# A gated mix of an S4 convolution and a routed FFN: a new order of the operations, and more, shorter idle matmuls at the start

## The chip, the core and the metric

The kernel runs on one core of a Trainium2 chip. The metric is the device time of one execution in microseconds. The engines are named as in the profile: PE (TensorE, matmuls; PEld is its weight load), DVE (VectorE), ACT (ScalarE), POOL (GpSimd) and SP (SyncE, which here only issues DMAs). "SPq" and "POOLq" are the DMA queues of SP and POOL. L574 is line 574 of the kernel before; where a line of the changed kernel is meant, that is said.

## The reference

```python
x = A_u                                             # 1 x 2048 x 512, bf16
g = sigmoid((x * gate_w).sum(-1, keepdims=True))
# a: S4 long convolution, D = 512 channels, N = 128 complex modes, L = 2048
dt = exp(log_dt)[:, None]; A = A_re + 1j * A_im
dB = dt * (B_re + 1j * B_im)
P = exp((dt * A)[:, :, None] * arange(L))
K = einsum("dn,dnl,dn->dl", C_re + 1j * C_im, P, dB).real
a = irfft(rfft(u, 2 * L) * rfft(K, 2 * L))[:L] + u * Dskip
# b: the two tokens with the largest x @ w_r go through a SwiGLU FFN
r = x @ w_r; idx = argsort(-r)[:2]; xs = x[idx]
y = (silu(xs @ w_gate) * (xs @ w_up)) @ w_down      # 512 -> 1792 -> 512
b = x.at[idx].add(y * sigmoid(r[idx]))
out = g * a + (1 - g) * b
```

## The kernel before

The convolution is done in the frequency domain with matrices held in DRAM. The sequence has two blocks of 1024 tokens (index j, or m where the input is transformed), and the channels two halves of 256 (index c). The stages are: the loads; the **turning of the parameters**; their polar form (exponentials and logarithms); the forward transform of u (`fw`, L872); the routing (`log`, L746, and `gmax`, with a few small matmuls at L769 to L772); the powers of the modes as phases and moduli, coarse and fine (phases on PE at L683 and L688, sines on ACT at L436, products on DVE at L407); the kernel's lags (L925, L939) and its spectrum (L964, L966); the product with the spectrum of u (`ac`, L1032 to L1036); the inverse transform (`iv`, L1111 and L1116); and its eviction with the gate's factor (`ive`, on ACT at L1127 or on DVE at L1131) with the outputs behind (L1135, L1137, L1139). The two FFN rows are worked out in the middle and scattered into a copy of x; the residual enters the inverse through a diagonal matrix `rd` (L1155 on).

**The turning** concerns this change most. The six parameter arrays A, B and C (real and imaginary) lie in DRAM with the channels in rows. `nat` (L526) loads each of them as 128 x 512, and `cia` (L524) loads a unit matrix `CI` from `c_id`. A matmul with that matrix turns a block of 128 x 128. `turned` (L569) does four such matmuls for each term, one for every fourth channel, so its results lie four words apart in PSUM. `nt1` and `nt0` turn the two arrays of A. `nw0` and `nw1` turn the products of B and C that DVE has made (`bc`, L580 on; each has two terms, hence eight matmuls). On DVE, `al`, `bs` and `bn` make the modes from `nt`, and `kw` (an L407 on 128x1024 from PSUM) takes the result of `nw0` and `nw1`.

**Idle matmuls** (`hm`, L533): PE multiplies a tile of ones into a PSUM tile `twm` that nobody reads. There are eight operations of two matmuls with 512 columns each.

**What sets the order.** Each operation is recorded by `P.add` or a helper (`MM` for PE, `TT` and `EV` for others, `DMA`), with the buffers that it reads and writes, and with one or two alternatives, that is, engines that can do it. A table `PLAN` then gives the order: a list of pairs, the operation's number as recorded and the alternative to use. A table `BANKS` gives the PSUM bank of each tile. `replay` (L128) applies both; `emit_plan` (L152) makes an instruction stream for each engine, in the order of PLAN, with the semaphore waits that the buffers demand. So every engine, and every DMA queue, runs its own part of PLAN strictly in order. Numbers such as `0.43`, `rate=` and `issue=` in the calls are the costs by which PLAN was searched; the chip doesn't see them.

Of the kernel before, what the change touches and what calls it, by code (L numbers as in the profile page):

```python
# [179 lines left out]
PLAN = [(4, 0), (0, 0), (5, 0), (6, 0), (3, 0), (1, 0), (2, 1), (21, 1), (30, 0), (22, 0), (23, 1), (13, 0), (34, 0), (14, 0), (39, 0), (82, 0),  # L180
# [37 lines left out]
L, D, NS, NF = 2048, 512, 128, 1792  # L218
# [100 lines left out]
def bass_gated_mix__ssm_conv_s4__moe_arch_mod__prompt_kernel(nc, A_u, A_A_re, A_A_im, A_B_re, A_B_im, A_C_re, A_C_im, A_log_dt, A_Dskip,  # L319
# [42 lines left out]
    with ExitStack() as es:  # L362
# [162 lines left out]
        def nat(i):  # L525
            DMA("nat%d" % i, lambda h: [h.dma_start(NAT(0, 128, i * 512, (1, 512)), dr(prm[i], 0, (4 * NS, 128), (1, 4 * NS)))], [], [bNAT[i]], 128, rate=250.0, also=(ACT,))  # L526
# [6 lines left out]
        def hm(h):  # L533
            r = None
            for k in range(2):
                r = h.matmul(P32(twm, 0, 0, 128, 0, (1, 512)), ONE(0, 128, 0, (1, 128)), ONE(0, 128, 0, (0, 4), (1, 128)), start=True, stop=True)
# [706 lines left out]
```

## Time and profile before

| | |
|---|---|
| median of 3 runs | 150.3 us (149.78 to 150.49) |
| profiled execution | 148.79 us, its span 146.8 us |
| granted TensorE clock | 1.00 |
| busiest group, L407 on DVE, all shapes | x120, 112.9 us |
| next, L427 on ACT (evictions) | x45, 37.8 us |
| next, L436 on ACT (sines) | x37, 36.7 us |
| moved by DMA | 26.46 MB, mean 180 GB/s |

The busy time of an engine, its share of the span and its number of instructions stand in the first line of the page behind the span. Behind that, the page cuts the span into 40 equal slices (3.67 us each) with one digit for each, the busy share in tenths:

```profile
PE   6597599899998989999879998859998999999990
DVE  0579999999999999999999999999999999999961
ACT  4599989999999999979665889999999552354650
PEclk9999999999999999999999999999999999999999
```

DVE reads 0 in the first and 6 and 1 in the last two slices, and 9 in nearly all between them. ACT falls to 2 to 6 in the last eight. A row of the waits view names an engine and what it worked on, then `<-` and the engine and the line for which it waited, then the idle us in sum, how often, and the longest. A row of the timeline gives the start and the time from there to the end of the last instruction of the row, then engine, line, shapes, the count (x8), and in brackets the idle time before it with what ended it.

### The profile page before, as it was taken

Reading aid. Unit: us, or ns where it says so; the run is one execution under the profiler, and the core shown is the slowest. Engines: PE = TensorE matmul, PEld = TensorE weight load, DVE = VectorE, ACT = ScalarE, POOL = GpSimd, SP = SyncE. Lnnn points to the kernel's source line nnn. Section 1 sums busy time; section 2 is a strip of 40 time slices with the busy share of each in tenths; the row PEclk is TensorE's granted clock in tenths of the full one; section 3 lists DMA queues with packets and bytes.
Section 4 is the critical chain, followed back from the end, with each engine's and each line's share of the span. In section 5 each row is a group of like instructions: output and inputs, shape, how many; then the busy total and the mean of one; then the engine's idle time right before and its main releaser. Section 6 shows DMA issues by size and latency. Waiting matters only on the chain.

```text
span 146.8 us, 3152 instructions
## 1 busy us (share of the span) xinstructions
PE 129.9 (88%) x1303; PEld 88.7 (60%) x1303; DVE 134.0 (91%) x173; ACT 116.2 (79%) x170; POOL 21.0 (14%) x30
## 2 busy tenths in 40 slices
PE   6597599899998989999879998859998999999990
PEld 1382275354345654775537876747886667778880
DVE  0579999999999999999999999999999999999961
ACT  4599989999999999979665889999999552354650
POOL 1000000621000549787000002000000000000000
PEclk9999999999999999999999999999999999999999
DMA  4999989999488559946996423553300039100167
GB/s 126 221 229 275 272 262 373 407 339 302 161 286 302 133 165 325 270 177 114 181 419 240 144 90 105 114 150 136 22 0 0 0 95 295 42 0 4 38 180 213
DMA packets 23710, 26.46 MB, mean 180 GB/s; under 512 B 9193, under 2 KB 20081, under 8 KB 23537
## 3 DMA queue, kind: packets, MB, share of 16 engines
q1 hardware_dynamic: 22174, 23.78, 52.5%
q0 software_dynamic: 1088, 2.10, 8.2%
q10 hardware_dynamic: 434, 0.39, 0.9%
q8 instruction: 10, 0.16, 0.5%
q14 instruction: 4, 0.02, 0.1%
HBM read 19.85 MB, written 4.20 MB: 164 GB/s over the span
## 4 chain that ended last, share of the span: by engine, by line
DVE 48%; PE 32%; ACT 8%; DMA 5%; issue 3%; SPq 1%
DVE RB L407 37%; PE psm L1116 11%; ACT RB L427 8%; PE psm L964 6%; PE psm L1032 4%; DVE RB L433 3%; DMA RB<-c_near 3%; DMA RB<-in_A_C_im_dram 3%; PE psm L574 2%; PE psm L1111 2%; PE psm L939 2%; DVE RB L708 2%; PE psm L1034 2%; PE psm L1036 2%; DVE RB L861 2%
## 5 line engine op out<-in xcount | busy, mean ns | idle before, releaser
L407 DVE TENSOR_TENSOR RB<-RB 128x2048 bf16<-128x2048 bf16 (+10 forms) x120 | 112.9, 987 | 1.8 <-DMA RB<-in_A_C_im_dram 0.4
L427 ACT ACTIVATE RB<-psm 128x1024 bf16<-128x1024 f32 (+7 forms) x45 | 37.8, 873 | 10.4 <-PE psm L1036 8.7
L436 ACT ACTIVATE RB<-psm 128x1024 bf16<-128x1024 int16 (+1 forms) x37 | 36.7, 1019 | 7.6 <-PE psm L688 2.9
L1116 PE MATMUL psm<-RB 128*128 128x256 bf16 x160 | 22.2, 273 | 0.0
L683 PE MATMUL psm<-RB 128*128 128x256 f16 (+1 forms) x112 | 20.7, 326 | 0.8 <-ACT RB L436 0.8
L436 ACT ACTIVATE RB<-RB 128x512 bf16<-128x512 f32 (+5 forms) x32 | 16.7, 591 | 2.2 <-DVE RB L407 2.1
L872 PE MATMUL psm<-RB 128*128 128x512 bf16 x64 | 16.1, 380 | 2.1 <-DVE RB L861 2.1
L1116 PEld LDWEIGHTS psm<-RB 128*128 128x128 bf16 x160 | 15.6, 98 | 1.9
L964 PE MATMUL psm<-RB 128*128 128x256 bf16 x128 | 15.1, 272 | 0.3 <-DMA RB<-c_near 0.3
L683 PEld LDWEIGHTS psm<-RB 128*128 128x128 f16 x112 | 10.4, 98 | 8.1 <-ACT RB L436 1.4
L964 PEld LDWEIGHTS psm<-RB 128*128 128x128 bf16 x128 | 12.4, 98 | 2.6 <-ACT RB L427 1.0
L688 PE MATMUL psm<-RB 128*128 128x512 f16 x44 | 12.6, 381 | 1.3 <-ACT RB L436 1.3
L1127 ACT ACTIVATE RB<-psm,RB 128x256 bf16<-128x256 f32 x25 | 10.2, 476 | 4.2 <-PE psm L1116 4.2
L872 PEld LDWEIGHTS psm<-RB 128*128 128x128 bf16 x64 | 5.8, 98 | 9.3 <-DVE RB L861 2.9
L925 PE MATMUL psm<-RB 128*128 128x80 bf16 x256 | 10.4, 198 | 0.8 <-ACT RB L427 0.4
L925 PEld LDWEIGHTS psm<-RB 128*128 128x128 bf16 x256 | 9.7, 96 | 2.4 <-ACT RB L427 1.2
L427 ACT ACTIVATE RB<-psm,RB 128x1024 bf16<-128x1024 f32 (+1 forms) x9 | 9.2, 1062 | 0.0
L1111 PE MATMUL psm<-RB 128*128 128x256 bf16 x32 | 8.7, 273 | 0.0
L574 PE MATMUL psm<-RB 128*128 128x128 bf16 x24 | 5.5, 493 | 2.3 <-DVE RB L407 1.9
L1032 PE MATMUL psm<-RB 128*128 128x512 bf16 x24 | 7.2, 380 | 0.3 <-DVE RB L407 0.3
L407 POOL TENSOR_TENSOR RB<-RB 128x1 f32<-128x1 f32 (+4 forms) x5 | 4.4, 879 | 20.4 <-DVE RB L843 19.4
L939 PE MATMUL psm<-RB 128*32 128x128 bf16 (+1 forms) x96 | 5.4, 391 | 2.2 <-ACT RB L427 2.2
(72 smaller groups left out, 124.8 us busy)
## 6 DMA issues: line engine op xcount, KB each, us to landing
RB<-in_A_u_dram SPq DMA_DIRECT2D x8, 256.0 KB, 5.9
RB<-RB POOLq DMA_DIRECT2D x4, 512.0 KB, 8.1
RB<-c_near SPq DMA_DIRECT2D x4, 512.0 KB, 4.8
RB<-c_inv SPq DMA_DIRECT2D x1, 2048.0 KB, 8.8
RB<-u_routed SPq DMA_DIRECT2D x2, 1024.0 KB, 5.6
RB<-in_B_w_up_dram SPq DMA_DIRECT2D x1, 1792.0 KB, 9.1
RB<-in_B_w_gate_dram SPq DMA_DIRECT2D x1, 1792.0 KB, 15.7
RB<-in_B_w_down_dram SPq DMA_DIRECT2D x1, 1792.0 KB, 8.3
```

The source lines that it names most:

```text
L407: return P.add(name, [(eng, c_dve(n, mode) if eng == DVE else 1.0, lambda h: h.tensor_tensor(out=o(), in0=a_(), in1=b_(), op=op))], rd, wr ...
L427: return lambda h: h.activation(out=o(), in_=a_(), func=ACTF.Copy, scale=scale() if callable(scale) else scale)
L436: return P.add(name, [(ACT, cost or c_act(n), lambda h: h.activation(out=o(), in_=a_(), func=func, scale=scale))], rd, wr, table=table, **kw)
L683: r = h.matmul(P32(t, 0, 0, 128, 256 * l0, (1, 256 * nl)), DGM(0, 128, (DD.index(d) + 2) * 128, (1, 128)), src(0, 128, col + hf * CW, (0, ...
L688: r = h.matmul(P32(t, b, 0, 128, 0, (1, 512)), DGM(0, 128, 0, (1, 128)), DGM(0, 128, 128 + c_, (0, 512)), start=False, stop=False, skip_gr ...
L872: x = h.matmul(P32(t, b, 0, 128, 0, (1, 512)), FM(0, 128, 2048 * par + 1024 * pl + 512 * i + 256 * q + 128 * b, (1, 128)), U(0, 128, ((m * ...
L925: x = h.matmul(P32(t, q // 6, 0, 128, (q % 6) * 80, (1, 80)), TPv(0, 128, ri * 16384 + c * 8192 + r * 128, (1, 128)), TQv(0, 128, c * 1024 ...
L964: x = h.matmul(P32(t, kt // 2, 0, 128, (kt % 2) * 256, (1, 256)), KN(0, 128, 2048 * KNP[2 * pl + hc] + 512 * g + 128 * kt, (1, 128)), KC[c ...
L1032: r = h.matmul(P32(t, kt, 0, 128, 0, (1, 512)), CI(0, 128, 0, (1, 128)), f(k, 0, 512), start=(k == 0 and hc == 1), stop=False, skip_group_ ...
L1111: h.matmul(o, RD(0, 128, (tb + 8) % 16 * 128, (1, 128)), UE[q](0, 128, r * 256, (1, 256)) if early else U2(0, 128, tb * D + c * CW, (1, 25 ...
L1116: x = h.matmul(o, G(0, 128, (pl * 4 + kt) * 1024 + (r * 2 + q) * 128, (1, 128)), PQ(0, 128, r * 1024 + kt * 256 + pl * 256 if quarter else ...
L1127: x = h.activation(out=OT[k](0, 128, ocol(q, r), (1, 256)), in_=P32(t, 0, 0, 128, q * 256, (1, 256)), func=ACTF.Copy, scale=SGF["gc"](0, 1 ...
```

## The change

It has four parts.

1. PLAN and BANKS are replaced by newly searched ones, with 558 operations where there were 541. The search used other costs for the first loads (`rate`, in GB/s): 200 for `cia` and `nat` where it had 250, 300 for `u` (350), 180 for the forward matrix `fm` (200), 220 for `cf` (none before).
2. There are 22 idle operations of one matmul with 256 columns each. `nw0` also reads `twm`, so that all of them stand ahead of it on PE.
3. For the first channel half and second block (c=0, j=1), the outputs go by residue r of the token number modulo 4: four DMAs of 128 KB instead of one operation with two DMAs of 256 KB each.
4. Outputs by residue may be issued by ACT as well as by SP.

```diff
-PLAN = [(4, 0), (0, 0), (5, 0), (6, 0), (3, 0), (1, 0), (2, 1), (21, 1), (30, 0), (22, 0), (23, 1), (13, 0), (34, 0), (14, 0), (39, 0), (82, 0),
...
+PLAN = [(0, 0), (4, 0), (5, 0), (6, 0), (7, 0), (8, 0), (9, 0), (10, 0), (11, 0), (12, 0), (13, 0), (14, 0), (3, 0), (27, 0), (1, 1), (48, 0),
...
-        DMA("cia", ..., rate=250.0, also=(ACT,))
+        DMA("cia", ..., rate=200.0, also=(ACT,))
...
         def hm(h):
-            r = None
-            for k in range(2):
-                r = h.matmul(P32(twm, 0, 0, 128, 0, (1, 512)), ONE(0, 128, 0, (1, 128)), ONE(0, 128, 0, (0, 4), (1, 128)), start=True, stop=True)
-            return r
-        for k in range(8):
-            MM("hm", hm, [bONE], [twm], 0.43)
+            return h.matmul(P32(twm, 0, 0, 128, 0, (1, 256)), ONE(0, 128, 0, (1, 128)), ONE(0, 128, 0, (0, 2), (1, 128)), start=True, stop=True)
+        for k in range(22):
+            MM("hm", hm, [bONE], [twm], 0.109)
...
-            MM(nm, f, rd + [bCIA], [t], 0.125 * 4 * len(terms))
+            MM(nm, f, rd + [bCIA] + ([twm] if nm == "nw0" else []), [t], 0.125 * 4 * len(terms))
...
-                if fin and (r != 3 or not last):
-                    DMA("out", ... [ob], [], 128)
+                if (fin or j) and (r != 3 or not last):
+                    DMA("out", ... [ob], [], 128, issue=0.55, rate=290.0, also=(ACT,))
             if last:
-                DMA("out", ... bo[3:], [], 128)
+                DMA("out", ... bo[3:], [], 128, issue=0.55, rate=290.0, also=(ACT,))
-            elif not fin:
+            elif not fin and not j:
```

The rows below are instructions in the order of one engine, with line, operation, result, operands and shape; x8 stands for eight alike in a row. The lines of the changed kernel are shifted by up to two.

The start of PE's stream, up to the forward matmuls. Before (L536 idle, L541 the step `dt`, L574 the turning, L737 a small product for the routing, L872 the forward transform, L599 and L600 two steps of the polar form):

```order
L536 MATMUL psm<-RB 128x512 x4
L541 MATMUL psm<-RB 128x512
L574 MATMUL psm<-RB 128x128 x24
L737 MATMUL psm<-RB 128x2 x4
L872 MATMUL psm<-RB 128x512 x8
```

and in the changed kernel (L535 idle, L539 `dt`, L572 the turning, L735 the small product, L597 and L598 the polar form):

```order
L535 MATMUL psm<-RB 128x256 x10
L539 MATMUL psm<-RB 128x512
L572 MATMUL psm<-RB 128x128 x8
L535 MATMUL psm<-RB 128x256 x10
L735 MATMUL psm<-RB 128x2 x4
L535 MATMUL psm<-RB 128x256 x2
L572 MATMUL psm<-RB 128x128 x16
L597 MATMUL psm<-RB 128x512
```

The turning's 24 matmuls stood together; now twelve idle ones and the small product stand between the first 8 (`nt`) and the last 16 (`nw`), and before the first 8 stand ten idle ones of half the width in place of four.

The start of SP's queue. Before (L524 is `cia`, L526 a parameter array, L551 a half of u, L553 half of the forward matrix, L445 the transposed load `xt` of u for the routing, the others small or diagonals):

```order
L526 DMA RB<-in_A_A_re_dram 128x512
L524 DMA RB<-c_id 128x256
L565 DMA RB<-in_A_Dskip_dram 1x512
L526 DMA RB<-in_A_B_im_dram 128x512
L566 DMA RB<-c_f 128x160
L526 DMA RB<-in_A_C_im_dram 128x512
L564 DMA RB<-in_B_w_r_dram 1x512
L553 DMA RB<-c_fwd 128x2048
L551 DMA RB<-in_A_u_dram 128x2x512 x2
L564 DMA RB<-in_gate_w_dram 1x512
L445 DMA_TRANSPOSE RB<-in_A_u_dram 128x4x2048
```

and in the changed kernel (L527 is a parameter array, L551 the forward matrix, L549 u, L446 `xt`):

```order
L527 DMA RB<-in_A_A_re_dram 128x512
L527 DMA RB<-in_A_A_im_dram 128x512
L527 DMA RB<-in_A_B_im_dram 128x512
L527 DMA RB<-in_A_C_im_dram 128x512
L562 DMA RB<-in_gate_w_dram 1x512
L527 DMA RB<-in_A_B_re_dram 128x512
L562 DMA RB<-in_B_w_r_dram 1x512
L527 DMA RB<-in_A_C_re_dram 128x512
L551 DMA RB<-c_fwd 128x2048
L549 DMA RB<-in_A_u_dram 128x2x512 x4
L551 DMA RB<-c_fwd 128x2048
L446 DMA_TRANSPOSE RB<-in_A_u_dram 128x4x2048
```

All six parameter arrays now come by SP's queue and `c_id` by ACT's, where SP had `c_id` and three of the arrays and ACT the other three; `xt` follows both halves of u's first block and of the forward matrix instead of one half of each. Farther down, half of u's second block follows the gate's weights (`w_gate`), which it preceded.

The end of ACT's stream. Before (L427 evicts products for the inverse, L1127 evicts outputs):

```order
L1127 ACTIVATE RB<-psm,RB 128x256 x2
L427 ACTIVATE RB<-psm 128x2x512
L1127 ACTIVATE RB<-psm,RB 128x256 x15
```

and in the changed kernel (L1125 evicts outputs, L1133 and L1135 issue them):

```order
L1125 ACTIVATE RB<-psm,RB 128x256 x6
L1133 DMA out_dram<-RB 128x2x256
L1125 ACTIVATE RB<-psm,RB 128x256 x4
L1133 DMA out_dram<-RB 128x2x256
L1125 ACTIVATE RB<-psm,RB 128x256 x4
L1133 DMA out_dram<-RB 128x2x256
L1125 ACTIVATE RB<-psm,RB 128x256 x2
L1133 DMA out_dram<-RB 128x2x256
L1125 ACTIVATE RB<-psm,RB 128x256
L1135 DMA out_dram<-RB 128x2x256
```

Five of the outputs, the last one among them, have moved from SP's queue to ACT's, between its evictions.

Some operations with two alternatives have changed engine. From ACT to DVE went four evictions of 128x1024 (L433 and L427 are the two engines' lines for an eviction), one of 960 columns, one of 768, one of 32x512, `sgc`, a copy, and `rd` of the first block. From DVE to ACT went five evictions of 1024, one of 960, one of 32x512, a change of sign (L708) and a small copy. Of the output evictions as many went one way as the other.

More of the change, by code (lines that the diff above doesn't have):

```diff
@@ L523, in bass_gated_mix__ssm_conv_s4__moe_arch_mod__prompt_kernel @@
         DMA("ldt", lambda h: [h.dma_start(LDT(0, 1, 0, (1, D)), dr(A_log_dt, 0, (D, 1), (1, D)))], [], [bLDT], 1, eng=ACT, first=2900.0)
-        DMA("cia", lambda h: [h.dma_start(CI(0, 128, 0, (1, 256)), dr(id_c, 0, (640, 128), (1, 256)))], [], [bCIA], 64, rate=250.0, also=(ACT,))
+        DMA("cia", lambda h: [h.dma_start(CI(0, 128, 0, (1, 256)), dr(id_c, 0, (640, 128), (1, 256)))], [], [bCIA], 64, rate=200.0, also=(ACT,))
         def nat(i):
-            DMA("nat%d" % i, lambda h: [h.dma_start(NAT(0, 128, i * 512, (1, 512)), dr(prm[i], 0, (4 * NS, 128), (1, 4 * NS)))], [], [bNAT[i]], 128, rate=250.0, also=(ACT,))
+            DMA("nat%d" % i, lambda h: [h.dma_start(NAT(0, 128, i * 512, (1, 512)), dr(prm[i], 0, (4 * NS, 128), (1, 4 * NS)))], [], [bNAT[i]], 128, rate=200.0, also=(ACT,))
         nat(1)
@@ L550, in ul @@
             for par in pars:
-                DMA("u%d" % m, lambda h, par=par: [h.dma_start(U(0, 128, m * 4096 + 2048 * q + 512 * par, (1024, 2), (1, 512)), dr(A_u, (m * BLK + 512 * q + par) * D, (4 * D, 128), (2 * D, 2), (1, D))) for q in range(2)], [], [bU[m][par]], 512, n=2, issue=0.92, also=also, rate=350.0)
+                DMA("u%d" % m, lambda h, par=par: [h.dma_start(U(0, 128, m * 4096 + 2048 * q + 512 * par, (1024, 2), (1, 512)), dr(A_u, (m * BLK + 512 * q + par) * D, (4 * D, 128), (2 * D, 2), (1, D))) for q in range(2)], [], [bU[m][par]], 512, n=2, issue=0.92, also=also, rate=300.0)
         def fl(par, also=()):
-            DMA("fm", lambda h: [h.dma_start(FM(0, 128, 2048 * par, (1, 2048)), dr(f_c, 2048 * par, (4096, 128), (1, 2048)))], [], [bF[par]], 512, also=also, rate=200.0)
+            DMA("fm", lambda h: [h.dma_start(FM(0, 128, 2048 * par, (1, 2048)), dr(f_c, 2048 * par, (4096, 128), (1, 2048)))], [], [bF[par]], 512, also=also, rate=180.0)
         for par in (1, 0):
@@ L565, in bass_gated_mix__ssm_conv_s4__moe_arch_mod__prompt_kernel @@
         DMA("dsr", lambda h: [h.dma_start(DSR(0, 1, 0, (1, D)), dr(A_Dskip, 0, (D, 1), (1, D)))], [], [bDSR], 1, eng=SP)
-        DMA("cf", lambda h: [h.dma_start(CF(0, 128, 0, (1, 160)), cf_c[:, :])], [], [bCF], 80, also=(ACT,))
+        DMA("cf", lambda h: [h.dma_start(CF(0, 128, 0, (1, 160)), cf_c[:, :])], [], [bCF], 80, rate=220.0, also=(ACT,))
         DMAT("xt", lambda: XT(0, 128, 0, (L, 4), (1, L)), lambda: dr(A_u, 0, (D, L), (1, D)), [bXT], 2048, issue=8.1, lat=2.5)
@@ L1133, in inverse @@
                 bo.append(ob)
-                if fin and (r != 3 or not last):
-                    DMA("out", lambda h, r=r: [h.dma_start(dr(out, (BLK * j + r) * D + c * CW, (4 * D, 128), (512 * D, 2), (1, CW)), OT[k](0, 128, ocol(0, r), (1024, 2), (1, 256)))], [ob], [], 128)
+                if (fin or j) and (r != 3 or not last):
+                    DMA("out", lambda h, r=r: [h.dma_start(dr(out, (BLK * j + r) * D + c * CW, (4 * D, 128), (512 * D, 2), (1, CW)), OT[k](0, 128, ocol(0, r), (1024, 2), (1, 256)))], [ob], [], 128, issue=0.55, rate=290.0, also=(ACT,))
             if last:
-                DMA("out", lambda h: [h.dma_start(dr(out, (BLK * j + 3) * D + c * CW, (4 * D, 128), (512 * D, 2), (1, CW)), OT[k](0, 128, ocol(0, 3), (1024, 2), (1, 256)))], bo[3:], [], 128)
-            elif not fin:
-                DMA("out", lambda h: [h.dma_start(dr(out, (BLK * j + 512 * q) * D + c * CW, (4 * D, 128), (D, 4), (1, CW)), OT[k](0, 128, ocol(q, 0), (256, 4), (1, 256))) for q in range(2)], bo, [], 512, n=2, issue=1.0)
+                DMA("out", lambda h: [h.dma_start(dr(out, (BLK * j + 3) * D + c * CW, (4 * D, 128), (512 * D, 2), (1, CW)), OT[k](0, 128, ocol(0, 3), (1024, 2), (1, 256)))], bo[3:], [], 128, issue=0.55, rate=290.0, also=(ACT,))
+            elif not fin and not j:
+                DMA("out", lambda h: [h.dma_start(dr(out, (BLK * j + 512 * q) * D + c * CW, (4 * D, 128), (D, 4), (1, CW)), OT[k](0, 128, ocol(q, 0), (256, 4), (1, 256))) for q in range(2)], bo, [], 512, n=2, issue=1.1, rate=290.0)
         coarse(0)
```

4 lines of the change are left out of this document (2 added, 2 removed), and 67 rows, old and new, of the table PLAN.

## The prediction

> **What bounds the kernel now.** I read the page first: the busy shares and the chain that ended last. Then the waits of DVE, and then the timeline of the two ends, since that is where DVE waits.
>
> ```profile
> span 146.8 us, 3152 instructions
> PE 129.9 (88%) x1303; PEld 88.7 (60%) x1303; DVE 134.0 (91%) x173; ACT 116.2 (79%) x170; POOL 21.0 (14%) x30
> DVE 48%; PE 32%; ACT 8%; DMA 5%; issue 3%; SPq 1%
> ```
>
> ```profile
> DVE RB L407 <- PE psm L574: 6.2, 2, 4.9
> DVE RB L1131 <- PE psm L1116: 1.6, 3, 0.8
> DVE RB L407 <- DMA RB<-in_A_C_im_dram: 0.4, 1, 0.4
> DVE RB L407 <- PE psm L1036: 0.3, 1, 0.3
> DVE RB L407 <- ACT RB L427: 0.2, 1, 0.2
> ```
>
> The profiled execution took 148.79 us, 2.0 over its span. DVE is busy 134.0 of 146.8; of the 12.8 idle, 4.9 lie ahead of its first operation, 1.2 (6.2 less 4.9) in a second wait for the turning of the parameters (L574), 1.6 between the last evictions, and 3.0 behind its last operation. In between it waits for 0.5 us in all. So DVE's list of work is the bound, and a change helps by what it takes off that list, off its head or off its tail. Each us added to the list costs a us.
>
> ```profile
> 0.99 1.89 PE L536 MATMUL psm<-RB 128*128 128x512 bf16 x4 [0.99 <-POOL RB L531]
> 3.79 1.89 PE L574 MATMUL psm<-RB 128*128 128x128 bf16 x8 [0.38 <-DMA RB<-c_id]
> 7.59 3.59 PE L574 MATMUL psm<-RB 128*128 128x128 bf16 x16 [1.92 <-DVE RB L407]
> 11.71 1.90 PE L872 MATMUL psm<-RB 128*128 128x512 bf16 x8
> 4.93 0.69 DVE L407 TENSOR_TENSOR RB<-RB,psm 128x512 f32<-128x512 bf16 x1 [4.93 <-PE psm L574]
> 5.71 0.69 DVE L424 SCALAR_TENSOR_TENSOR RB<-RB,psm 128x512 f32<-128x512 bf16 x1
> 6.84 1.29 DVE L407 TENSOR_TENSOR RB<-RB 128x1024 bf16<-128x1024 bf16 x2 [0.44 <-DMA RB<-in_A_C_im_dram]
> 9.58 0.42 DVE L430 CAST RB<-RB 128x512 f16<-128x512 f32 x1
> 11.23 1.22 DVE L407 TENSOR_TENSOR RB<-psm,RB 128x1024 bf16<-128x1024 f32 x1 [1.23 <-PE psm L574]
> 12.37 0.42 DVE L417 TENSOR_SCALAR RB<-RB 128x512 int32<-128x512 f32 x1
> ```
>
> Here the array shows two rates: four matmuls of 512 columns take 1.89 us at 0.99, eight take 1.90 at 11.71. So it runs at half rate at first, though the page's granted clock reads 9 in every slice. The 16 turning matmuls at 7.59 are spaced by 0.213 us (3.59 less the last one's length of about 0.4, over 15), and "kw" on DVE at 11.23 waits for them.
>
> **Term 1, the head: -1.3 us.** `nt0` cannot start before `c_id` has landed. That load goes from SP's second issue at 1.18 to ACT's second, where one stood at 1.30: +0.1. From "al" on, DVE's list before `kw` is now al, bs, bn, bc, bc, bn2, i124, i256, hi. From the rows' starts and lengths that is 0.78 + 0.69 + 0.35 + 1.2 + 0.6 + 0.35 + 0.34 + 0.42, about 4.8 us, so DVE is ready for `kw` at 9.85, with i256 behind it (which stood at 12.37 and cost 0.33). The bc products must find all four B and C loads landed at about 6.75. The last is SP's eighth issue, at about 3.4 (issues are 0.4 apart), with less ahead of it than the load that landed at 6.82; I hold this at 0, with 0.3 as its bad end.
>
> On PE, `nt0` and `nt1` end at about 5.6. Ten idle matmuls at 0.21 (half of the 0.42 at 0.99) follow to 7.7, then `wl` and two more to 8.1, then 16 turning matmuls. Since the array will have been busy without a gap for over 4 us by then, and it had reached the full rate at 11.71 after 3.6 busy us, I take the full rate here: half of 0.213, so 1.7 us, and 0.3 for the last one's way: `kw` at 10.2. The gain is 1.03 and the 0.33 of i256. No row has these matmuls at full rate. The near end is the plain 128-column matmul below, spaced by 0.055 ((0.38 - 0.22)/3): then DVE's 9.85 sets the start and the gain is 1.7. The far end is the 0.213 of now: turning ends at 11.8, `kw` starts 0.3 later than the old start plus i256, a loss of 0.3. I take 1.3 (1.36, rounded for the later load), as both plain kinds of matmul halve.
>
> ```profile
> 72.46 2.69 PE L939 MATMUL psm<-RB 128*32 128x128 bf16 x48 [0.58 <-ACT RB L427]
> 75.61 0.38 PE L834 MATMUL psm<-RB 128*2 128x128 bf16 x4
> ```
>
> [...]
>
> **Term 2, DVE's list: +1.0 us.** The order also picks the engine of each two-engine operation again. Eleven leave DVE for ACT and twelve come.
>
> ```profile
> L433 DVE CAST RB<-psm 128x1024 bf16<-128x1024 f32 x3 | 3.7, 1220 | 0.0
> L433 DVE CAST RB<-psm 128x960 bf16<-128x960 f32 x2 | 2.3, 1149 | 0.0
> L433 DVE CAST RB<-psm 32x512 bf16<-32x512 f32 x1 | 0.7, 696 | 0.0
> L1159 ACT ACTIVATE RB<-RB 128x128 bf16<-128x128 bf16 x16 | 4.9, 393 | 0.0
> L605 DVE TENSOR_TENSOR RB<-RB 128x1024 f32<-128x1024 bf16 x1 | 1.2, 1219 | 0.0
> L708 DVE TENSOR_SCALAR RB<-RB 128x1024 bf16<-128x1024 bf16 x8 | 3.3, 412 | 0.0
> L413 DVE TENSOR_SCALAR RB<-RB 128x512 f32<-128x512 f32 x1 | 0.4, 419 | 0.0
> ```
>
> Leaving: five evictions of 1024 (5 x 1.22), one of 960 (1.15), one of 32x512 (0.70), a sign change (L708, 0.41), a small copy (0.17): 8.5. Coming: four of 1024 (4.88), one of 960 (1.15), one of 32x512 (0.70), one of 768 (between the rows of 512 and 960: 0.95), `rd`, the diagonal of the residual, 1024 elements with an f32 operand (as L605: 1.22; on ACT it was 8 of L1159's 16), `sgc` (as L413 0.42, or up to 0.69), a copy (0.16): 9.6. The evictions of the outputs change places one for one. The difference is 1.1, less the 0.08 by which neighbours overlap. What ACT is spared is worth nothing, since ACT is idle 21%. With DVE idle for 0.5 us inside, nothing hides the added work; if all those waits went it would be +0.5, and +1.1 with the slow `sgc`.
>
> **Term 3, the tail: -0.5 us.**
>
> ```profile
> 136.68 3.15 DVE L407 TENSOR_TENSOR RB<-RB 128x1024 bf16<-128x1024 bf16 x4
> 143.37 0.42 DVE L1131 TENSOR_TENSOR RB<-psm,RB 128x256 bf16<-128x256 f32 x1 [0.29 <-PE psm L1116]
> 141.91 2.25 SPq L1135 DMA_DIRECT2D out_dram<-RB  x4
> 144.26 0.43 SPq L1137 DMA_DIRECT2D out_dram<-RB  x1
> ```
>
> From DVE's last product at 139.83 to the end at 146.84 pass 7.0 us: 3.5 of matmuls, the last eviction to 143.79, then 0.47 until the last output is issued, as SP is at the four before it until 144.16. In the new order ACT issues that one, with its previous issue about 2 us earlier, so nothing stands ahead of it: -0.4. PE has one matmul of 0.11 less behind the last product: -0.1. Four issues of about 0.45 now stand between ACT's evictions; ACT's two evictions and one issue in the last 3.2 us take 1.8, so they are covered. If that cover fails, the term is 0; at best 0.9, since PE is almost without a gap from 116 on and has less left there.
>
> **What else moves: 0.** On SP the transposed load `xt` now follows both halves of `u` and `fm` instead of one each, 1 MB more.
>
> ```profile
> 5.96 10.65 SPq L445 DMA_TRANSPOSE RB<-in_A_u_dram  x1
> RB<-in_A_u_dram SPq DMA_TRANSPOSE x1, 12.7
> 14.00:16.00 2.00, 0.16 (x2) 0.02 (x2) 2.00 (x5) 1.77 (x4) 0.00 (x0) 1.00 1.28 290
> 22.64 0.50 SPq L804 DMA_DIRECT2D RB<-in_B_w_gate_dram  x1
> RB<-in_B_w_gate_dram SPq DMA_DIRECT2D x1, 1792.0 KB, 15.7
> ```
>
> `xt` landed at 18.7; at 290 GB/s the extra MB makes it about 22.5. Then come `log` on PE (2.3 us) and the first phases (1.5), to about 26.5; the first sine stands on ACT behind three evictions that end near 28.5, so 2 us cover it. The first half of `u1` now stands behind `wg`. The same queue had moved as many bytes by about 33; PE needs it by 37, ahead of a small matmul that DVE waits for: 4 us of cover, less if the loads lag. The two outputs of (0,1) become four, two queues apart, under products.
>
> **The sum:** -1.3 + 1.0 - 0.5 = -0.8. Execution 148.0, span 146.0. The median shown is 1.5 above the profiled execution, so I predict 150.3 - 0.8 = **149.5 us**.
>
> **Rivals.**
> *The turning does not get faster.* Its output steps by four words in PSUM (`(4, 128)` in L574's function), and so does that of L939, which ran when the array was long at full rate. Its 48 matmuls take 2.5 us: 0.25 for each four of 128 columns. If the four run side by side, a stepped one takes longer at full rate than the turning does now; if one after the other, 0.06. Against it: L536 and L872 halve. Price: `kw` at 11.85, term 1 is +0.3, the sum +0.8: **151.1**, slower. It decides where the spacing stays above 0.16, as there the sum is nil.
> [...]
> *The parts cancel.* The full rate comes in the midst of the turning, or the tail keeps its 0.5 as the last transfers share engines: term 1 at -0.6 or term 3 at 0, sum about -0.2: **150.1**.
> *A load comes late.* `u1` at 39 instead of 33: PE and then DVE stand for 2 us, sum +1.2: **151.5**. For it: `wg` took 15.7 us to land when other weights were ahead of it. Against it: those are now behind.
> *More goes right.* Full rate before 8 and the inner waits gone: -1.7, **148.6**.
>
> **How the numbers follow.** 0.5% is about what a measurement can tell here: 149.55 to 151.05 count as the same. The forecast (-0.4 to -1.3) gets 0.40, the better case 0.10, cancelling 0.20, turning unchanged 0.20, a late load 0.10. Faster: 0.10, with about 0.32 of the forecast's 0.40 (its side below 149.55 and what the waits would add): 0.42. Slower: most of the two slow cases, 0.25. The same: 0.33. The range leaves out a fifth at the ends: 147.9 (the three terms at their good ends, -1.7 + 0.5 - 0.9 = -2.1, and 0.3 for the runs' own spread, 149.78 to 150.49) to 151.6 (turning unchanged and 0.5 more from loads).
>
> **What would show it.** Right: turning matmuls spaced by about 0.11 and `kw` on DVE before 10.5; DVE busy at about 135.0; the last output issued within 0.15 us of the last eviction. Wrong: the turning (L572 in the changed kernel) still spaced by 0.213; a wait of DVE over 0.5 us between 15 and 60 us, behind the forward matmuls or the small matmuls of the routing on PE; the sine of ACT starting later than 30. A median over 151.1 would mean that a wait I hold at nothing decides.

## The result and the profile after

The changed kernel takes 148.08 us (median of 17 runs), the kernel before 149.78 (17 runs). The ratio is 0.9926, with a 95% interval of 0.9898 to 0.9954, so the gain is 1.1 us (0.7 to 1.5); the two medians alone lie 1.7 apart. The forecast was a gain of 0.8, or 149.5 us after a median of 150.3. The profiled execution took 148.18 us, 0.61 less than that of before. In the experiments below, each group of four shares a chip. In the second group one execution of the kernel before ran at 146.87 us, 1.2 below its next, and as a ratio leaves out what is over 1.5% above the fastest, 15 of its 23 executions fell out; so that group's ratios are not used, and its medians are held against one another.

The page of the changed kernel: span, busy times, the slices of DVE and of the granted clock, and the chain.

```profile
span 146.4 us, 3151 instructions
PE 128.3 (88%) x1302; PEld 89.0 (61%) x1309; DVE 135.5 (93%) x174; ACT 114.5 (78%) x162; POOL 18.1 (12%) x30
DVE  0699999989999999999999999999999999999962
PEclk9999999689999999999999999999999999999999
DVE 44%; PE 33%; ACT 18%; issue 3%; POOL 0%; DVEq 0%; POOLq 0%
```

DVE is busy for 1.5 us more, and the chain now runs through ACT for 18% of the span (8% before). A new thing stands in the clock: 6 and 8 in the eighth and ninth slice. DVE's waits:

```profile
DVE RB L408 <- PE psm L572: 4.9, 1, 4.9
DVE RB L1129 <- PE psm L1114: 1.4, 4, 0.6
DVE RB L770 <- PE psm L769: 0.4, 1, 0.4
DVE RB L408 <- ACT RB L437: 0.2, 1, 0.2
```

The second wait for the turning and the one for C_im are gone; one behind the routing (L770) is new. The timeline of the start:

```profile
0.99 2.31 PE L535 MATMUL psm<-RB 128*128 128x256 bf16 x10 [0.99 <-POOL RB L532]
5.37 1.68 PE L535 MATMUL psm<-RB 128*128 128x256 bf16 x10
7.50 1.92 PE L572 MATMUL psm<-RB 128*128 128x128 bf16 x16
6.76 1.89 DVE L408 TENSOR_TENSOR RB<-RB 128x1024 bf16<-128x1024 bf16 x3
9.70 1.22 DVE L408 TENSOR_TENSOR RB<-psm,RB 128x1024 bf16<-128x1024 f32 x1
```

At half rate, at 0.99, ten idle matmuls take 2.31 us; the ten at 5.37 take 1.68, and the spacing within them halves at about 6.2 (0.213 us to 0.109), so the full rate comes there. The 16 turning matmuls then take 1.92 us instead of 3.59. Start to start they stand 0.109 us apart (0.213 before), and `kw` on DVE runs at 9.70 instead of 11.23, without a wait. And of the end:

```profile
143.56 0.42 DVE L1129 TENSOR_TENSOR RB<-psm,RB 128x256 bf16<-128x256 f32 x1 [0.18 <-PE psm L1114]
144.07 0.38 ACTq L1135 DMA_DIRECT2D out_dram<-RB  x1
```

The last output is issued 0.09 us after DVE's end (143.98) where it was 0.47.

DVE's time can be written as a ledger, in us, each item worked out from its rows of the timeline:

| | before | after | |
|---|---|---|---|
| idle up to `kw`, gaps over 0.09 | 6.60 | 4.91 | -1.69 |
| busy | 133.95 | 135.45 | +1.50 |
| idle between `kw` and the last evictions | 0.50 | 0.95 | +0.45 |
| idle between the last evictions | 1.56 | 1.36 | -0.20 |
| gaps under 0.09 | 1.17 | 1.29 | +0.12 |
| from DVE's end to the end of the span | 3.04 | 2.42 | -0.62 |
| span | 146.8 | 146.4 | -0.4 |

So in this pair of profiles the list and the new waits gave the gain at the head back, and the tail is what was left. The medians differ by more. The experiments ask why, and which part of the change does what.

### The profile page after: what moved, and what is told of

Its sections match the earlier page's. It is cut to its first block, busy times and chain, and to the rows that moved or that the text cites. A ratio compares the mean times of both kernels' runs of the same rounds, so it can differ in the third digit from the quotient of the medians.

```text
span 146.4 us, 3151 instructions
## 1 busy us (share of the span) xinstructions
PE 128.3 (88%) x1302; PEld 89.0 (61%) x1309; DVE 135.5 (93%) x174; ACT 114.5 (78%) x162; POOL 18.1 (12%) x30
## 4 chain that ended last, share of the span: by engine, by line
DVE 44%; PE 33%; ACT 18%; issue 3%; POOL 0%; DVEq 0%; POOLq 0%
DVE RB L408 36%; ACT RB L437 11%; PE psm L1114 10%; ACT RB L428 6%; PE psm L962 5%; PE psm L1030 4%; DVE RB L434 3%; PE psm L1109 2%; PE psm L937 2%; PE psm L1034 2%; PE psm L1032 2%; DVE RB L706 2%; PE psm L535 2%; PE psm L681 1%; ACT L1186 1%
## 5 line engine op out<-in xcount | busy, mean ns | idle before, releaser
L408 DVE TENSOR_TENSOR RB<-RB 128x2048 bf16<-128x2048 bf16 (+8 forms) x120 | 113.0, 987 | 1.4 <-ACT RB L437 0.2
L681 PE MATMUL psm<-RB 128*128 128x256 f16 (+1 forms) x112 | 21.1, 336 | 0.2 <-ACT RB L428 0.2
L870 PE MATMUL psm<-RB 128*128 128x512 bf16 x61 | 15.0, 383 | 5.8 <-ACT RB L428 3.8
L686 PE MATMUL psm<-RB 128*128 128x512 f16 x44 | 13.5, 393 | 2.8 <-ACT RB L437 2.8
L681 PEld LDWEIGHTS psm<-RB 128*128 128x128 f16 x112 | 10.8, 101 | 8.0 <-issue 0.5
L1125 ACT ACTIVATE RB<-psm,RB 128x256 bf16<-128x256 f32 x25 | 10.2, 472 | 5.2 <-PE psm L1114 4.2
L923 PE MATMUL psm<-RB 128*128 128x80 bf16 x256 | 10.4, 198 | 0.5 <-ACT RB L428 0.4
L686 PEld LDWEIGHTS psm<-RB 128*128 128x128 f16 x44 | 3.5, 100 | 6.7 <-ACT RB L437 5.9
L1030 PE MATMUL psm<-RB 128*128 128x512 bf16 x21 | 6.5, 380 | 0.8 <-ACT RB L428 0.6
L883 POOL DMA_DIRECT2D RB<-RB x2 | 2.6, 1321 | 32.6 <-ACT RB L428 32.6
L434 DVE CAST RB<-psm 128x1024 bf16<-128x1024 f32 (+3 forms) x6 | 6.4, 1062 | 0.0
## 6 DMA issues: line engine op xcount, KB each, us to landing
RB<-c_inv SPq DMA_DIRECT2D x1, 2048.0 KB, 10.4
```

The lines of the kernel that those rows point to most:

```text
L408: return P.add(name, [(eng, c_dve(n, mode) if eng == DVE else 1.0, lambda h: h.tensor_tensor(out=o(), in0=a_(), in1=b_(), op=op))], rd, wr ...
L434: return P.add(name, [(ACT, c_act(n), f_act(o, a_)), (DVE, c_dve(n, 1), lambda h: h.tensor_copy(o(), a_()))], rd, wr, **kw)
L681: r = h.matmul(P32(t, 0, 0, 128, 256 * l0, (1, 256 * nl)), DGM(0, 128, (DD.index(d) + 2) * 128, (1, 128)), src(0, 128, col + hf * CW, (0, ...
L686: r = h.matmul(P32(t, b, 0, 128, 0, (1, 512)), DGM(0, 128, 0, (1, 128)), DGM(0, 128, 128 + c_, (0, 512)), start=False, stop=False, skip_gr ...
L870: x = h.matmul(P32(t, b, 0, 128, 0, (1, 512)), FM(0, 128, 2048 * par + 1024 * pl + 512 * i + 256 * q + 128 * b, (1, 128)), U(0, 128, ((m * ...
L923: x = h.matmul(P32(t, q // 6, 0, 128, (q % 6) * 80, (1, 80)), TPv(0, 128, ri * 16384 + c * 8192 + r * 128, (1, 128)), TQv(0, 128, c * 1024 ...
```

## The experiments

### The kernel before, once more

> The kernel before, unchanged, for a second profile and the clock of each run. Theory (its time differs from run to run because the array reaches the full rate at differing points of the head): turning matmuls (L574) spaced by 0.213 us again or partly, kw on DVE anywhere from 10.0 to 12, and executions that differ by up to 2 us at a granted clock of 1.0. Rival (the differences come from elsewhere, for instance loads): kw at 11.2 within 0.1 whatever the time of the run. Time: ratio 1.00.

149.69 us, ratio 1.002 (0.9989 to 1.0051). Its profiled execution took 149.62, 0.83 more than the first. The timeline of DVE at the start:

```profile
4.75 0.69 DVE L407 TENSOR_TENSOR RB<-RB,psm 128x512 f32<-128x512 bf16 x1 [4.75 <-PE psm L574]
7.13 1.29 DVE L407 TENSOR_TENSOR RB<-RB 128x1024 bf16<-128x1024 bf16 x2 [0.91 <-DMA RB<-in_A_C_im_dram]
11.51 1.22 DVE L407 TENSOR_TENSOR RB<-psm,RB 128x1024 bf16<-128x1024 f32 x1 [1.23 <-PE psm L574]
```

The turning is at half rate again, and its wait is 1.23 to the hundredth. What differs is the wait for C_im: 0.91 us here, 0.44 in the profile on which the prediction was built. That profile was one of the better executions. So the rival was right for these two profiles: the rate of the turning does not make the difference between them, though `kw` did move, by 0.28, with the load. It can do so in others: in the profile of the kernel without its late idle matmuls, below, the last turning matmuls ran at full rate (3.22 us for the 16 instead of 3.59) and the wait was 0.85.

### Only the idle matmuls at the head, in the old order

```diff
-        for k in range(8):
-            MM("hm", hm, [bONE], [twm], 0.43)
+        for k in range(20):
+            MM("hm", hb if 2 <= k < 14 else hm, [bONE], [twm], 0.43)
...
+        at_nw0 = plan.index((49, 0))
+        plan[at_nw0:at_nw0] = [(7 + k, 0) for k in range(12)]
```

`hb` is the changed kernel's idle matmul of 256 columns; (49, 0) is `nw0`.

> The kernel before, its order untouched, with only twelve idle matmuls of 256 columns added between the turning of A and that of B and C. Theory (the idle matmuls alone bring the head's gain): turning of B and C spaced by about 0.11 us instead of 0.213, kw on DVE at 10.0 to 10.2 instead of 11.23, time 1.0 to 1.4 us less than before. Rival A (the gain needs the new order of the loads): kw stays above 11. Rival B (what DVE gains at the head it loses again in waits for the late halves of u and the forward matrix, which land at 21.7 and 23.9): kw early, but at most 0.4 us less.

148.59 us against 149.34, ratio 0.9973 (0.9945 to 1.0000). The timeline of the head:

```profile
5.25 2.85 PE L539 MATMUL psm<-RB 128*128 128x256 bf16 x12
7.89 2.15 PE L576 MATMUL psm<-RB 128*128 128x128 bf16 x16
7.00 1.29 DVE L407 TENSOR_TENSOR RB<-RB 128x1024 bf16<-128x1024 bf16 x2 [0.74 <-DMA RB<-in_A_C_im_dram]
10.07 1.23 DVE L407 TENSOR_TENSOR RB<-psm,RB 128x1024 bf16<-128x1024 f32 x1
```

`kw` at 10.07 without a wait: the idle matmuls alone do that, so rival A falls. The 0.74 for C_im stays. The gain, by the ratio 0 to 0.8 us, is smaller than the theory's 1.0 to 1.4; by the interval rival B's size fits, though no wait for a late load shows in this profile. (More on this at the end of the experiments.)

### The changed kernel with idle matmuls of two columns

```diff
-P32(twm, 0, 0, 128, 0, (1, 256)), ONE(0, 128, 0, (1, 128)), ONE(0, 128, 0, (0, 2), (1, 128))
+P32(twm, 0, 0, 128, 0, (1, 2)), ONE(0, 128, 0, (1, 128)), ONE(0, 128, 0, (1, 2))
```

> The changed kernel with its idle matmuls cut from 256 columns to 2. Theory: turning of B and C back at 0.213 us, kw at about 11.3 instead of 9.70, and 1.2 to 1.7 us more than the changed kernel (0.1 to 0.7 more than before). Rival (the earlier kw is owed to the order of the loads and of DVE's list): kw still below 10.2 and the time of the changed kernel within 0.4 us.

149.28 us, ratio to before 1.0013 (0.9979 to 1.0048); next to the changed kernel's 0.9926 that is 1.3 us more, as the theory had it.

```profile
8.08 3.60 PE L572 MATMUL psm<-RB 128*128 128x128 bf16 x16 [0.66 <-DVE RB L408]
11.72 1.23 DVE L408 TENSOR_TENSOR RB<-psm,RB 128x1024 bf16<-128x1024 f32 x1 [1.36 <-PE psm L572]
```

The turning is back at 3.60 us and DVE waits 1.36. Without its idle matmuls the whole new order is worth nothing measurable. The profiled execution (150.70) is one of the two slowest of twelve: in it DVE waits another 1.2 us, for ACT, behind a stretch of half rate that begins at 56.7.

### The kernel before without its late idle matmuls

The prediction did not count something that the change takes away: in the old order six of the eight idle operations stand at 16.9 to 24.4 us, around the routing's 64 small matmuls. Here (`hs`) they have two columns.

```diff
-            MM("hm", hm, [bONE], [twm], 0.43)
+            MM("hm", hm if k < 2 else hs, [bONE], [twm], 0.43)
```

> The kernel before with its six late idle operations (at 16.9 to 24.4 us, around the routing's 64 small matmuls) cut from 512 columns to 2; the two at the start stay. Theory (these kept the array at the full rate, and the change took them away): the granted clock falls to about 0.5 for some 3.4 us between 20 and 30, as in the changed kernel at 26.6, mean clock 0.98 to 0.99, and 0.3 to 0.9 us more than before. Rival (the half rate in the changed kernel comes from its longer wait of PE at 17.8 to 21.5 only): clock stays at 1.00 and the time is that of before within 0.3.

149.19 us, ratio 0.9979 (0.9948 to 1.0011). A windows view gives, for each stretch, the busy time and count of PE, PEld, DVE, ACT and POOL, then the granted clock, the DMA share and GB/s:

```profile
17.00:20.00 3.00, 1.93 (x23) 1.15 (x23) 3.00 (x4) 3.00 (x6) 0.00 (x0) 0.59 1.15 297
20.00:23.00 3.00, 3.00 (x64) 2.65 (x63) 3.00 (x6) 2.48 (x6) 0.00 (x0) 0.50 0.82 240
```

The theory was right on the clock, 0.50 where it had been 1.00, and wrong on the time: DVE is busy in all 6 us of it, and in the old order this costs nothing.

### The changed kernel with all outputs on SP

```diff
-        P.replay(PLAN, BANKS)
+        P.replay([(i, 0 if P.ops[i].name == "out" else a) for i, a in PLAN], BANKS)
```

> The changed kernel with all its outputs issued by SP. Theory (the shorter tail, 2.4 us from DVE's end to the span's end instead of 3.0, is owed to the last output being issued by ACT): the last output is issued 0.3 to 0.6 us later after DVE's last eviction than in the changed kernel, and the time is 0.3 to 0.6 us above the changed kernel's. Rival (SP would have been free as well, and the issues on ACT delay its evictions): same time within 0.2, or less.

148.08 us, the median that the changed kernel had as well (on another chip). The timeline of its end:

```profile
144.36 0.42 DVE L1129 TENSOR_TENSOR RB<-psm,RB 128x256 bf16<-128x256 f32 x1 [0.18 <-PE psm L1114]
144.86 0.37 SPq L1135 DMA_DIRECT2D out_dram<-RB  x1
```

The last output is issued 0.08 us after DVE's end (144.78), and the span ends at 147.2, again 2.4 later. The theory falls: ACT's issues bring nothing. SP is free in time: its last outputs begin at 133.85, while in the kernel before they begin at 137.28 and the operation with two large DMAs (L1139) stands among them at 140.53.

This profile, of 148.98 us, shows something else. From 49.9 to 53.4 us, right behind 56 matmuls of two columns (L808, 48.1 to 49.7), the array runs at half rate (the number ahead of the last two is the granted clock), and then DVE waits for a sine on ACT:

```profile
51.00:52.00 1.00, 1.00 (x3) 0.30 (x2) 1.00 (x1) 0.97 (x2) 0.00 (x0) 0.50 0.00 0
DVE RB L706 <- ACT RB L437: 1.0, 1, 1.0
```

Ten phase matmuls (L681) take 4.00 us there, against 2.32 in the changed kernel's first profile. The wait begins at 56.8. No profile of the old order has such a wait of over 0.35 us between 15 us and its last evictions.

### The changed kernel with idle matmuls around the routing

```diff
+        twl = P.pst(1, "hl")
+        for k in range(6):
+            MM("hl", lambda h: h.matmul(P32(twl, 0, 0, 128, 0, (1, 512)), ONE(...), ..., start=True, stop=True), [bONE], [twl], 0.22)
...
+        plan[at_log + 1:at_log + 1] = [(31, 0), (32, 0)]
+        plan[at_log:at_log] = [(27 + k, 0) for k in range(4)]
```

> The changed kernel with six idle matmuls of 512 columns in a free PSUM bank, four just ahead of the routing's 64 small matmuls and two behind them. Theory A (the half rate from 26.6 us comes of the stretch of small matmuls): granted clock at 1.00 in all slices around 26, no wait of ACT for the first phases at 28.5 (0.90 before) and none of DVE at 30.9 (0.41); the fill itself puts the small matmuls back by 0.9, so the time is between 0.6 less and 0.2 more than the changed kernel. Theory B (it comes of PE's wait at 17.8 to 21.5, before the fill): the half rate stays, and the time is 0.3 to 0.9 above.

149.41 us, 1.3 more than the kernel with its outputs on SP in the same group.

```profile
21.69 4.45 PE L873 MATMUL psm<-RB 128*128 128x512 bf16 x12 [3.74 <-ACT RB L428]
25.98 1.03 PE L540 MATMUL psm<-RB 128*128 128x512 bf16 x4
26.84 2.25 PE L747 MATMUL psm<-RB 128*128 128x2 bf16 x64
```

Here the half rate came ahead of the fill: twelve forward matmuls took 4.45 us behind PE's wait of 3.74, where the changed kernel's profile has 2.76. The fill then only put the routing back (26.84 instead of 25.69 with the outputs on SP, where the forward matmuls took 4.31 and DVE did not wait for it), and DVE waited 0.99 us. So for this stretch B (the cause is the wait at 17.8 to 21.5) fits, though the loss is larger than its 0.3 to 0.9. Theory A was not put to the test: it concerns a half rate that sets in behind the small matmuls, as at 26.6 in the first profile, and here there was none. To fill PE's wait itself was not tried.

### The changed kernel with the residual's diagonal on ACT

```diff
+        rd0 = next(o.i for o in P.ops if o.name == "rd")
-        P.replay(PLAN, BANKS)
+        P.replay([(i, 1 if i == rd0 else a) for i, a in PLAN], BANKS)
```

> The changed kernel with the first block's residual diagonal (rd, 1.21 us on DVE at 82 us) back on ACT, as eight small activations of some 0.39 us. Theory (DVE's list is the bound and ACT has slack there): DVE busy 134.2 instead of 135.5, and 0.9 to 1.2 us less than the changed kernel. Rival (ACT's 3.1 us delay its evictions of the spectrum, on which DVE's products wait): a new wait of DVE of over 0.5 us between 84 and 100, and less than 0.4 us gained, or a loss.

151.54 us is the median of six; two of them took 157.2 at a granted clock of 0.945, and the other four have 151.06, some 3 us more than the kernel with its outputs on SP. DVE is busy 134.7 and waits for ACT:

```profile
DVE RB L408 <- ACT RB L428: 3.4, 4, 1.5
```

One of them, 0.96 us up to 84.82, comes ahead of the activations, just behind the place where DVE had `rd`; so most of the 1.2 us taken off its list is lost at once. Then the timeline of ACT:

```profile
88.61 2.43 ACT L1157 ACTIVATE RB<-RB 128x128 bf16<-128x128 bf16 x8
90.95 1.00 ACT L428 ACTIVATE RB<-psm 128x1024 bf16<-128x1024 f32 x1
```

The rival was right. The eight small activations take 2.43 us, of which ACT was idle for 0.72 at this place in the changed kernel. They put back by 1.5 us the eviction of the spectrum, and DVE waits 1.47 for it at 90.5.

### Only two small loads moved, in the old order

```diff
+        plan = [p for p in PLAN if p[0] not in (30, 31)]
+        k = plan.index((24, 0)) + 1
+        plan[k:k] = [(31, 0), (30, 0)]
```

Operation 30 is the load of Dskip, 31 that of the f32 constants (`c_f`), 24 that of C_im. In the changed kernel these two also stand late in SP's queue, behind all the parameter arrays and the first `c_fwd`; the list of its start above leaves them out:

```profile
4.57 0.43 SPq L564 DMA_DIRECT2D RB<-c_f  x1
5.05 0.30 SPq L563 DMA_DIRECT2D RB<-in_A_Dskip_dram  x1
```

> The kernel before with only two small loads (Dskip and the f32 constants) moved behind the last parameter array in SP's queue, so that C_im is issued 0.8 us earlier. Theory (DVE's wait for C_im ahead of the products B x C, 0.44 to 0.91 in three profiles of the kernel before, is owed to this issue and is what the new load order takes away beside the idle matmuls): the wait falls to 0.2 or less, the turning of B and C starts as much earlier, still at 0.213 us, and the time is 0.3 to 0.8 below before. Rival (the loads share their rate, so C_im lands when it did): wait 0.4 or more, time as before.

148.29 us against 149.56 by the medians. It was measured again in the third group:

> The kernel before with only the two small loads behind C_im, once more, since the comparison of the first time was blurred. Theory: wait for C_im 0.2 or less, kw some 0.5 to 0.9 earlier than in the kernel before, and 0.5 to 1.3 us below before. Rival: within 0.3 of before.

148.81 us against 149.56, ratio 0.9955 (0.9918 to 0.9992). The first run's timeline of DVE:

```profile
5.98 1.29 DVE L407 TENSOR_TENSOR RB<-RB 128x1024 bf16<-128x1024 bf16 x2
10.36 1.22 DVE L407 TENSOR_TENSOR RB<-psm,RB 128x1024 bf16<-128x1024 f32 x1 [1.23 <-PE psm L574]
```

And the second run's:

```profile
5.53 0.69 DVE L407 TENSOR_TENSOR RB<-RB,psm 128x512 f32<-128x512 bf16 x1 [5.53 <-PE psm L574]
11.29 1.22 DVE L407 TENSOR_TENSOR RB<-psm,RB 128x1024 bf16<-128x1024 f32 x1 [1.23 <-PE psm L574]
```

No wait for C_im in either run, and `kw` waits its 1.23 as before. The theory holds for the wait. The head is shorter in the first profile only: there DVE's first operation starts at 4.49 and `kw` at 10.36. In the second the first operation comes at 5.53, as `c_id` landed 3.2 us after its issue (2.1 in the first), and `kw` stands at 11.29, no earlier than before. So that the time falls rests on the two medians and the ratio, and by how much depends on how the loads land.

### Both small edits, and then the outputs by residue as well

> The kernel before with the two small edits together: Dskip and the f32 constants issued behind C_im, and ten idle matmuls of 256 columns between the two turnings; everything else in its old order, with the idle matmuls around 17 to 24 us kept. Theory (the change's whole gain at the head comes of these two, and the rest of the new order gives back more than it brings): no wait of DVE for C_im or for the turning over 0.3, kw at about 9.2 to 9.6, granted clock at 1.00 between 10 and 60 us, DVE busy 134.0, and 1.6 to 2.4 us below before, so 0.2 to 1.0 below the changed kernel. Rival (the two gains hide one another, or DVE then waits for later loads): not more than 1.3 below before.

148.38 us, ratio 0.9941 (0.9913 to 0.9970), 0.9 us below before. In the profile both waits are gone, but DVE gives 0.47 back soon after:

```profile
9.62 1.22 DVE L407 TENSOR_TENSOR RB<-psm,RB 128x1024 bf16<-128x1024 f32 x1
DVE RB L863 <- PE psm L874: 0.5, 1, 0.5
```

It waits for the forward matmuls, which stand on PE behind the small product; PE waits 2.15 us, until 11.53, for that product's load of `gate_w`. The measured gain is about half of what the theory had, and the rival's bound (1.3) and its wait for a later load hold. Then the outputs by residue on top, with each of the four placed behind its own eviction:

```diff
-                if fin and (r != 3 or not last):
+                if (fin or j) and (r != 3 or not last):
...
-            elif not fin:
+            elif not fin and not j:
```

> The same as the kernel with the two small edits, and the outputs of the first half's second block by residue (four of 128 KB, each behind its own eviction) instead of two of 256 KB at the end, all still by SP. Theory (the shorter tail of the changed kernel comes of this, not of ACT's issues): last output issued within 0.15 us of DVE's end instead of 0.46, 2.4 us from DVE's end to the span's end instead of 3.0, and 0.3 to 0.7 us less than without it. Rival (the tail is set by the last transfer's own way): 0.2 or less.

147.26 us (6 runs), ratio 0.9835 (0.9791 to 0.9878). The end of its timeline:

```profile
142.07 0.42 DVE L1133 TENSOR_TENSOR RB<-psm,RB 128x256 bf16<-128x256 f32 x1 [0.29 <-PE psm L1118]
142.65 0.42 SPq L1139 DMA_DIRECT2D out_dram<-RB  x1
```

The last issue comes 0.16 us after DVE's end (142.49), and the span ends 2.5 after it (3.0 without this edit). The two profiled executions differ by 0.49 (147.61 and 147.12), as expected, of which the tail has 0.5; at the head `kw` is later here (10.15, behind a wait of 0.34), and in return the 0.47 is missing. The ratios differ by 1.6 us, the medians by 1.1. With three small edits of the old order, five of its six executions (147.04 to 147.71) lie below all eight of the changed kernel (147.88 and more):

> The changed kernel unchanged, beside the others on the same chip: 1.0 to 1.7 us below before. Theory on its clock (the array falls to half rate for stretches of 3.4 us after its longer idle times ahead of 22 us, at places that differ from run to run): mean clock 0.96 to 0.99, with the profile's half-rate stretch again between 12 and 30 us but not at the same place. Rival (the drop stands at a fixed place of the program): again at 26.6.

On the same chip the changed kernel has 148.13 us, ratio 0.9882 (0.9844 to 0.9919). Its profiled execution took 148.88, 0.70 more than the first. Windows of this one:

```profile
20.00:23.00 3.00, 1.42 (x4) 0.58 (x5) 3.00 (x4) 2.97 (x5) 0.00 (x0) 0.62 1.07 277
23.00:26.00 3.00, 3.00 (x9) 1.06 (x7) 2.97 (x6) 2.97 (x5) 0.00 (x0) 0.50 0.97 227
26.00:29.00 3.00, 3.00 (x69) 2.46 (x67) 2.00 (x4) 2.43 (x3) 0.27 (x1) 0.75 0.94 361
```

and its waits of DVE:

```profile
DVE RB L431 <- PE psm L744: 1.0, 1, 1.0
```

By windows of 1 us, the half rate lasts from 20.7 to 27.5 us here, where the first profile had it from 26.6 to 30.0. The place is not fixed. DVE waits 1.0 us for the routing (L744), in the first one 0.4 (L769, behind it).

The record has the granted clock of every execution. One stretch of 3.4 us at half rate lowers the mean by about 0.012 (half of 3.4 in a span of 147):

| | at 0.996 or more | their median | lower | their median |
|---|---|---|---|---|
| before, first group | 26 of 35 | 149.29 us | 9 | 149.72 us |
| idle matmuls alone | 7 of 12 | 148.35 us | 5 | 149.33 us |
| before, third group | 18 of 23 | 149.56 us | 5 | 149.91 us |
| both small edits | 5 of 12 | 147.90 us | 7 | 149.03 us |
| both, and the outputs by residue | 3 of 6 | 147.12 us | 3 | 147.31 us |
| changed kernel, 17 and 8 executions | 1 of 25 | 148.64 us | 24 | 148.07 us |

Among the executions without a whole such stretch, the idle matmuls alone gain 0.9 us and both small edits 1.7, near what their theories had. The others of these two kernels take 1.0 to 1.1 us more, and they are more frequent than in the kernel before. So what was missing of the two gains goes with the half rate. That it is the cause is not shown: neither kernel was profiled in an execution with such a stretch.

## Why the prediction was right

**What bounds the kernel.** Right: the ledger of DVE gives the span, and the two runs that put a wait on DVE (`rd` on ACT, the fill) lost time. But taking work off the list is not worth its length everywhere: without `rd`, DVE waited 0.96 us just behind its place.

**Term 1, the head.** The mechanism was right and shown from both sides: idle matmuls alone in the old order bring the turning to full rate (2.15 us for the 16 instead of 3.59), and without them the new order loses it (3.60 instead of 1.92). The rival of the stepped output falls: at full rate it takes 0.109 us, half of 0.213. Only the size was off: forecast -1.3, the ledger -1.69. DVE was ready for `kw` at 9.70 where 9.85 was worked out, and PE was done by then (9.42), the near end of the term: the idle matmuls ended at 7.55 and not at 8.1, as the full rate came among them. In the five profiles with the changed kernel's idle matmuls the full rate came between 5.4 and 7.1, at 6.2 in the first, and within the turning, at about 8.4, in that of the idle matmuls in the old order (hence the 2.15 us). The prediction took it for granted only from 8.1 on: it counted its "over 4 us" without a gap from the turning at 3.8, against 3.6 in the kernel before, though PE had been at work from 0.99 on. How much work it takes was the prediction's estimate; the runs don't show what sets the moment, which differs by up to 1.7 us among the five.

**The loads.** "I hold this at 0" came true: no load makes DVE wait. But that the old wait for C_im goes is a gain, and the prediction sized it by the one execution that it had, at 0.44, within the 1.03 of `kw`. Three other profiles of the old order of loads have 0.91, 0.74 and 0.90, the new order none. That is a likely reason why the medians differ by more than the two profiled executions; moving two small loads alone gains 0.7 us (0.1 to 1.2).

**Term 2, DVE's list.** By the rows of the operations that changed engine it is +0.95, as forecast (+1.0). But DVE's busy time rose by 1.50. The lengths of all its rows add up to 144.95 and 145.61 us, only 0.66 more, as a small operation of 128x16 took 0.38 less, while the stretches that they cover are 133.95 and 135.45: neighbours overlap by 11.0 us before and by 10.2 after. The prediction's "less the 0.08" had this with the wrong sign. And "what ACT is spared is worth nothing" is too wide: on average ACT is idle (22% of the span), but with `rd` on ACT, 2.4 us of activations, the kernel took some 3 us more.

**Term 3, the tail.** Right in size, -0.5 forecast and -0.62 measured, and wrong in its reason. The step that failed is "In the new order ACT issues that one": with all outputs on SP nothing changes (2.4 us from DVE's end), and with outputs by residue in the old order the tail is as short (2.5).

**What else moves.** `xt` landed at 22.40, as worked out (22.5), and no load made DVE wait. The sum missed the idle matmuls that the change takes away behind 16 us. PE then waits some 3.7 us for evictions before 21.5, and runs at half rate for one or two stretches of 3.4 us around or after it. In the old order half rate at that place cost nothing (ratio 0.9979); in the new one DVE's wait behind the routing runs from none (outputs on SP) to 1.0 us, and two profiles have a later stretch with a wait of 1.0 and 1.2 behind it. In the changed kernel's second profile two of the signs that the prediction had named as wrong showed: a wait of DVE over 0.5 us behind the routing's small matmuls (0.99), and ACT's first sine later than 30 (30.35). Fill, order of the evictions and the clock were not taken apart further, so how much of the +0.45 belongs to the clock stays open.

So the forecast came out by a sum in which misses partly cancelled: the list and the new waits were worse by 0.95 (0.50 and 0.45 in the ledger), the head was better by 0.4 in the profile and, by an estimate from the waits for C_im (0.44 against 0.74 to 0.91), by about as much again in the median, for the loads. That the sum still fits is in part luck. As a time, 148.08 lies 1.4 below the forecast and just inside its range (147.9); 0.5 of that is the median of three executions from which it started, 150.3, where 17 have 149.78.

## What to carry to other kernels

Idle matmuls are worth having where a wait of the bounding engine ends on TensorE soon after the start (`kw` at 9.70 us instead of 11.23), and here they reached up to that work with hardly a gap; how much of a gap they stand was not tried. Before trusting one profile, take a second: a wait for a load that is 0.4 us in one execution and 0.9 in the next changes what an edit of the load order is worth. A searched order bundles gains and losses; undoing and adding its parts one at a time found three small edits that beat it by 0.7 us (by the ratios) to 0.9 (by the medians). And look at the granted clock of every execution beside its time: an edit that brings the head forward can be worth less in those where the array falls back to half rate later (here they took 1.0 to 1.1 us more).

## What the runs showed of the hardware that was not expected

The turning's matmuls, of 128 columns with an output that steps by four words in PSUM, stand 0.109 us apart at full rate and 0.213 at half rate. The plain idle matmuls of 256 columns have the same two spacings (L535 in the first profile after), and a plain one of 128 columns takes 0.055 at full rate (L834, in the prediction). So a column with the stepped output took twice as long here as one with a plain output, at either rate. The weight load that each of the turning's matmuls has does not set this: the idle matmuls have weights of 128x128 too, and so have 256 matmuls of 80 columns (L925), which are busy for 10.4 us, 0.041 each.

The page's granted clock reads 1.00 at the start, in which the array runs at half rate (the spacing of 0.213 up to 6.2 us in the first profile after, and to the end of the turning at 11.2 in the one before), but it does show later half rate (0.50 in the windows above). The spacing of equal matmuls is the safer reading at the start.

Six profiles have a wait of PE of 3.1 to 4.0 us that ends between 21.5 and 22.7. In five of them the half rate came within it or up to 1.1 us behind it (20.4 to 22.6), in one 5.1 us behind it (26.6). It lasts 3.4 us or, in two of them, 6.8, with PE busy for most of that. Where it sets in 5.1 us behind the wait, the last 2.3 us are the routing's 64 matmuls of two columns, and the stretch at 49.9 in the run with the outputs on SP also follows 56 such matmuls. In the old order, with the idle matmuls around the routing cut to two columns, the half rate lasts from 17.5 to 24.4. There it sets in ahead of the routing's matmuls, within a wait of PE (0.10 us busy from 17 to 18). Whether such small matmuls or the waits beside them bring the half rate was not shown; no run separates the two.
